# Two attention decodes on one core: the last weights in a staircase of transfers

## The chip, the cores and the metric

The kernel runs on one core of one Trainium2 chip. The metric is the device time of one execution in microseconds. An execution with the profiler gives the trace from which all rows in this document come.

## What is computed

There are two independent attention blocks, A and B, of the same size. Each decodes a single token against a cache of 8192 positions, with 32 heads of 128, and the two results are put side by side. All inputs are bfloat16.

```python
B, Sq, D = 1, 1, 512
H, Sk, Dh = 32, 8192, 128
q = (x @ wq).reshape(B, Sq, H, Dh).transpose(0, 2, 1, 3)
scores = einsum("bhqd,bhkd->bhqk", q, k_cache) * (Dh ** -0.5)
o = einsum("bhqk,bhkd->bhqd", softmax(scores), v_cache)
y = o.transpose(0, 2, 1, 3).reshape(B, Sq, H * Dh) @ wo
out = concatenate([yA, yB], axis=-1)
```

K and V of one block are 64 MB each, wq and wo 4 MB each, so that some 285 MB (decimal) go from HBM into the core once. The output has 1024 numbers.

## The kernel before, in words

Four heads of one block are handled together; I call this a quad. There are 16 quads (`NM`), numbers 0 to 7 of A and 8 to 15 of B. Each of the four heads takes 32 of the 128 partitions, and a partition holds 256 positions (`T`) of its head. So K or V of a quad is one transfer of 8 MB, 64 KB for each partition.

For a quad n the steps are: `plan_mul` multiplies K by the broadcast q on DVE, in four chunks of 64 columns; `plan_red` sums over the head dimension, first on PE with the identity as weights (L342), then on DVE (`plan_sr`, L353); `plan_max`, `plan_gmax` and `plan_exp` (L390, on ACT) make the softmax's numerators `pt`; `plan_sum` (L395) the denominators; `plan_pv` (L411) takes 256 column tiles of V as weights, with the four columns of `pt` as moving data; `plan_o` (L421) scales the result into `oD`. PV of quad n-1 is written between the chunks of quad n. K has two buffers, V has one.

All large loads are issued by SP, in the order in which `load_...` is called, and each waits on SP for its buffer. K of quad n+1 waits for the last reduction of quad n-1, and V of quad n waits for the end of PV of quad n-1. In the last round there is no K left to load; there the projection weights wo take the buffer of the K that was reduced last but one (`wo_sb`, L192): all of A and the first `BEFORE` groups of B are issued in K's place, ahead of the last V, and the other groups of B after it (L503 to L506, L536 and L537).

`WOG` (L169) divides the heads of wo into groups, (first head, number of heads). A group is one transfer (`load_wo`, L286) of 128 partitions: a row for each partition, n heads x 512 columns x 2 bytes, 1 KB for each head. In the matmul with wo the contraction runs over the partition, p, and partition p has n neighbouring rows of wo and not one row of each head. Therefore `oD` is regrouped for each group of more than one head (`plan_relayout`, L440): a masked product on DVE (L449), one matmul with a selection matrix (L454) and a copy (L458) into `o2`. `plan_wo` (L461) then does four matmuls for each head with wo as weights (L469), all accumulating in one PSUM bank, after a wait for the group's transfer (`s_wo[a][g]`). A group of one head is taken straight from `oD`. `plan_y` (L476) copies the sum into `yT` on DVE, and `plan_out` (L480) transposes it, copies it and stores it by SP.

Before the change B has eight groups, of 8, 4, 4, 8, 4, 2, 1 and 1 heads. The first two are issued ahead of the last V, the six others after it. The last V comes in three transfers (`VLAST`, L172), of columns 0 to 128, 128 to 192 and 192 to 256, each with a semaphore of its own, and `plan_pv` is cut at the same columns for each quad. The order on PE at the end is: the projection of A and of B's first two groups; the regrouping of the groups that need no head of the last quad; PV of quad 15 by parts; `plan_o`; the group after `BEFORE`; the regrouping of the group that does need the last quad (heads 28 and 29); the remaining groups in order; `yT`, out.

PE runs quads 1 to 15 as a loop over one body of instructions. PV of quad 15 takes the same body a second time with the rest left out (L581 to L599).

Of the kernel before, what the change touches and what calls it, by code (L numbers as in the profile page):

```python
# [11 lines left out]
P = 128  # L12
# [11 lines left out]
class _Plan:  # L24
# [15 lines left out]
    def op(self, eng, fn, ctr=None, needs=(), inc=1):  # L40

        for m in needs:
            self.wait(eng, m)
        self.prog[eng].append((fn, ctr, inc))
        if ctr is None:
            return None
        ctr.n += inc
        return ctr, ctr.n
# [81 lines left out]
def bass_concat_heads__mha_block_cached__gqa_block_cached__decode_kernel(  # L130
# [18 lines left out]
    NA = 2  # L149
# [9 lines left out]
    T = Sk // HP  # L159
    assert T == 256  # L160
    QA = H // G
    NM = NA * QA
    NK = 2
    CT = 64
    NCH = T // CT
    DW = 512 // CT
    assert Dh % DW == 0

    WOG = [[(0, 32)], [(0, 8), (8, 4), (12, 4), (16, 8), (24, 4), (28, 2), (30, 1), (31, 1)]]  # L169
    BEFORE = 2  # L170
    RG = [32, 16, 8, 4, 2]
    VLAST = (0, T // 2, T // 2 + CT, T)  # L172

    with ExitStack() as st:
        ec = st.enter_context
# [8 lines left out]
        def flat(ap):  # L184
            return ap.rearrange("p t d -> p (t d)")
# [6 lines left out]
        wo_sb = [flat(kn[:, KW])[:, a * W:(a + 1) * W].rearrange("p (j n) -> p j n", n=NOUT)  # L192
                 for a in range(NA)]
# [37 lines left out]
        def ctr(name):  # L231
            return _Ctr(nc, st, name)

        s_x = ctr("s_x")
        s_w = [ctr("s_w%d" % a) for a in range(NA)]
        s_wo = [[ctr("s_wo%d%d" % (a, i)) for i in range(len(WOG[a]))] for a in range(NA)]
        s_k = [ctr("s_k%d" % i) for i in range(NK)]
        s_v = [ctr("s_v%d" % i) for i in range(len(VLAST) - 1)]
        s_out = ctr("s_out")
# [3 lines left out]
        def dma(eng, dst, src, c, needs=()):  # L243
            return op(eng, lambda e: e.dma_start(dst, src), c, needs, inc=16)  # L244
# [21 lines left out]
        k_in, v_in, wq_in, wo_in = {}, {}, {}, {}  # L266
        red_done, pv_done, q_done, wo_done = {}, {}, {}, {}
# [9 lines left out]
        def load_v(n, cuts=(0, T)):  # L277
            dst, src = flat(vn[:]), quad(vs, n)
            v_in[n] = [(t0, dma("SP", dst[:, t0 * Dh:t1 * Dh], src[:, t0 * Dh:t1 * Dh], s_v[i],
                                [q_done[1] if n == 0 else pv_done[n - 1]]))  # L280
                       for i, (t0, t1) in enumerate(zip(cuts, cuts[1:]))]
# [4 lines left out]
        def load_wo(a, g):  # L286
            h0, n = WOG[a][g]
            src = wos[a][h0 * Dh:(h0 + n) * Dh, :].rearrange("(p j) n -> p (j n)", p=P)
            wo_in[a, g] = dma("SP", wo_sb[a][:, h0:h0 + n, :].rearrange("p j n -> p (j n)"), src,
                              s_wo[a][g], [red_done[NM - 2, NCH - 1]])  # L290


        for a in range(NA):
# [80 lines left out]
        def plan_exp(n):  # L374
            def bc(e):
                r = None
                for h in range(G):
                    r = e.matmul(bmp[:, 0:1], hrow[0:1, h, :], gm[0:1, h:h + 1],  # L378
                                 start=(h == 0), stop=(h == G - 1))
                return r  # L380
            m = op("PE", bc, c_pe, [i_pool, gm_done[n], nb_done.get(n - 1)])
            nb_done[n] = op("ACT", lambda e: e.activation(  # L382
                negb[:, n:n + 1], bmp[:, 0:1], AF.Copy, scale=-scale), c_act, [m])
            wait("ACT", nb_done[n])
            wait("ACT", pv_done.get(n - 1))
            wait("ACT", r_done.get(n - 1))
            wait("ACT", i_pool)
            for h in range(G):
                q = slice(h * HP, (h + 1) * HP)
                p_done[n] = op("ACT", lambda e, h=h, q=q: e.activation(  # L390
                    pt[q, :, h], s_sb[q, :], AF.Exp, bias=negb[q, n:n + 1],
                    scale=scale, accum_out=rsum[q, h:h + 1]), c_act)

        def plan_sum(n):
            m = op("PE", lambda e: e.matmul(misc[:, 0:G], ones_f[:], rsum[:],  # L395
                                            start=True, stop=True), c_pe,
                   [p_done[n], misc_free[0]])
            r_done[n] = misc_free[0] = op("DVE", lambda e: e.reciprocal(
                rinv[:, n, :], misc[:, 0:G]), c_dve, [m])

        def plan_pv(n, t0, t1):
            for t, landed in v_in[n]:
                if t < t1:
                    wait("PE", landed)
            wait("PE", p_done[n])
            wait("PE", o_done.get(n - 1))

            def mm(e):
                r = None
                for t in range(t0, t1):  # L410
                    r = e.matmul(acc[:, 0:G], vn[:, t, :], pt[:, t, :],  # L411
                                 start=(t == 0), stop=(t == T - 1))
                return r
            if t1 == T:
                pv_done[n] = op("PE", mm, c_pv)
            else:
                op("PE", mm)
# [22 lines left out]
        def plan_relayout(*groups):  # L440
            assert len(groups) <= 2
            made = []
            for a, g in groups:
                h0, n = WOG[a][g]
                z = z_n[0] % 2
                z_n[0] += 1
                s = P // n
                zv = zb[:, z, :].rearrange("p (h s) -> p h s", s=s)
                made.append((a, g, h0, n, z, op("DVE", lambda e, a=a, h0=h0, n=n, s=s, zv=zv: e.tensor_tensor(  # L449
                    zv, oD[:, a, h0:h0 + n].unsqueeze(2).broadcast_to([P, n, s]),  # L450
                    mask[n][:, None, :].broadcast_to([P, n, s]), ALU.mult),
                    c_dve, [sel_ready[n], o_done[a * QA + (h0 + n - 1) // G], z_free.get(z)])))
            for a, g, h0, n, z, m in made:
                z_free[z] = op("PE", lambda e, n=n, z=z: e.matmul(  # L454
                    z_ps[z][:, 0:n], zb[:, z, :], jsel[n][:], start=True, stop=True),
                    c_pe, [m, z_read[z][0]])
            for a, g, h0, n, z, m in made:
                o2_ready[a, g] = z_read[z][0] = op("DVE", lambda e, a=a, h0=h0, n=n, z=z: e.tensor_copy(  # L458
                    o2[:, a, h0:h0 + n], z_ps[z][:, 0:n]), c_dve, [z_free[z]])

        def plan_wo(a, g):  # L461

            h0, n = WOG[a][g]

            def mm(e):
                r = None
                for j in range(h0, h0 + n):
                    for i in range(NQ):
                        r = e.matmul(qyp[:, i:i + 1], wo_sb[a][:, j, i * P:(i + 1) * P],  # L469
                                     (o2 if n > 1 else oD)[:, a, j:j + 1], start=(j == 0 and i == 0),  # L470
                                     stop=(j == H - 1 and i == NQ - 1), skip_group_check=True)
                return r
            wo_done[a] = op("PE", mm, c_pe, [o2_ready[a, g] if n > 1 else o_done[a * QA + h0 // G],
                                            wo_in[a, g], qy_free[0]])
# [23 lines left out]
        for n in range(NM):  # L498
            if n >= L0:
                cuts[n].append(len(pl.prog["PE"]))  # L500
            if n + 1 < NM:
                load_k(n + 1)
            else:  # L503
                load_wo(0, 0)
                for g in range(BEFORE):
                    load_wo(1, g)  # L506
# [13 lines left out]
            else:  # L520
                cuts[n].append(len(pl.prog["PE"]))
                plan_sum(n - 1)
                for t0, t1 in zip(VLAST, VLAST[1:]):
                    plan_pv(n - 1, t0, t1)
# [6 lines left out]
            plan_exp(n)  # L531
            load_v(n, VLAST if n == NM - 1 else (0, T))
        cuts[NM].append(len(pl.prog["PE"]))
        NB = len(WOG[1])
        early = [g for g, (h0, n) in enumerate(WOG[1]) if h0 + n <= H - G]
        for g in range(BEFORE, NB):  # L536
            load_wo(1, g)  # L537
        z_read[1][0] = gm_done[NM - 1]
        plan_relayout((0, 0), (1, 0))
        plan_relayout((1, 1))  # L540
        plan_wo(0, 0)
        plan_y(0)
        for g in range(BEFORE):
            plan_wo(1, g)
        plan_relayout(*[(1, g) for g in early[BEFORE:BEFORE + 2]])
        plan_relayout(*[(1, g) for g in early[BEFORE + 2:]])
        wait("PE", misc_free[0])
        cuts[NM].append(len(pl.prog["PE"]))
        plan_sum(NM - 1)
        for t0, t1 in zip(VLAST, VLAST[1:]):  # L550
            plan_pv(NM - 1, t0, t1)
        cuts[NM].append(len(pl.prog["PE"]))
        plan_o(NM - 1)
        plan_wo(1, BEFORE)
        plan_relayout(*[(1, g) for g in range(len(early), NB) if WOG[1][g][1] > 1])
# [5 lines left out]
        for name, at in (("SP", block.sync), ("PE", block.tensor), ("ACT", block.scalar),  # L561
                         ("DVE", block.vector), ("POOL", block.gpsimd)):
            @at
            def _(e, name=name):
# [7 lines left out]
                final = _steps(prog[cuts[L1][1]:cuts[L1][2]])  # L572
                assert len(final) == b - a == len(VLAST)
                for k, (ws, it) in zip(range(a, b), final):
# [53 lines left out]
```

## Time and profile before

| What | Value |
|---|---|
| Median of two executions | 668.25 us (668.13 and 668.37) |
| The profiled execution | 668.1 us, its span 666.3 us |
| Granted PE clock over the span | 0.767 |
| Read from HBM | 285.21 MB, 428 GB/s over the span |
| Last K landed, first multiply of quad 15 | 604.9 us |
| Last V issued, three transfers | 631.58 us |
| Six groups of wo of B issued after it | from 632.90 us, 5.40 us in all |
| PV of quad 15, 192 tiles and 64 tiles | from 651.35 us for 5.29 us, from 657.50 us for 1.87 us |
| Last quad's `oD` | 659.40 us |
| `yT` of B | 663.91 us |
| Output store issued | 664.74 us |

Times within an execution are microseconds from the start of the span. The span ends with the last instruction; the profiled execution's own time is 1.8 us longer than its span. "Busy" is the time in which an engine had an instruction in it. A line such as `661.04 1.01 PE L469 ... x32 [0.82 <-DMA ...]` means: from 661.04 us on, for 1.01 us, PE ran 32 matmuls of line 469, and had stood idle for 0.82 us until a DMA came in. `SPq` is SP's queue of DMA issues. In the table by windows each row is a stretch of the span, with the busy time of each engine in it, the granted PE clock, the busy share of the 16 DMA engines and what they moved.

### The profile page before, as it was taken

The page shows a single profiled execution, that of the slowest core. Times are in us where ns is not written, and L with a number is a line of the kernel's source. Part 1 is how long each engine was busy: PE and PEld are TensorE (multiplying, and loading weights), DVE is VectorE, ACT ScalarE, POOL GpSimd, SP SyncE. Part 2 cuts the span into 40 slices and gives each one's busy share as a digit, 9 for nine tenths or more (in the row PEclk, how much of TensorE's full clock was granted, in tenths as well). Part 3 has the DMA queues.
Part 4 walks back from the last instruction along what each step waited for, and adds up shares of the span by engine and source line. Part 5 has one row for each costly group of instructions (what it writes and reads, how often), then busy time and mean ns, then how long its engine had stood idle before and what let it go on. Part 6 is the DMA issues. An engine that isn't in the chain of part 4 may idle for free.

```text
span 666.3 us, 12270 instructions
## 1 busy us (share of the span) xinstructions
PE 445.5 (67%) x5648; PEld 254.5 (38%) x5648; DVE 340.8 (51%) x219; ACT 62.4 (9%) x151; POOL 2.8 (0%) x15
## 2 busy tenths in 40 slices
PE   2065876848487594848659484865948386685866
PEld 1022352625244261614426161442626144252646
DVE  1095807466381836638082663809256481925611
ACT  1002002020201002020200202020020202002020
POOL 1000000000000000000000000000000000000000
PEclk9998767879787765978776587877658797765875
DMA  9999999999999999999999999999999999999997
GB/s 378 441 441 438 438 435 441 409 425 441 433 433 441 437 441 437 409 433 441 433 433 441 433 441 429 421 433 441 429 437 437 437 441 421 425 437 437 408 430 301
DMA packets 6509, 285.34 MB, mean 428 GB/s; under 512 B 738, under 2 KB 996, under 8 KB 1508
## 3 DMA queue, kind: packets, MB, share of 16 engines
q1 hardware_dynamic: 6496, 285.22, 99.2%
q8 instruction: 6, 0.10, 0.1%
q14 instruction: 3, 0.02, 0.0%
q10 hardware_dynamic: 4, 0.00, 0.0%
HBM read 285.21 MB, written 0.00 MB: 428 GB/s over the span
## 4 chain that ended last, share of the span: by engine, by line
DMA 57%; PE 28%; DVE 12%; issue 2%; SPq 1%; another core or an unknown queue 0%; ACT 0%
DMA kn<-in_B_k_cache_dram 20%; DMA kn<-in_A_k_cache_dram 18%; PE rps L342 17%; DVE kn L333 11%; PE acc L411 10%; DMA vn<-in_A_v_cache_dram 10%; DMA vn<-in_B_v_cache_dram 5%; DMA kn<-in_B_wo_dram 4%; DVE s_sb L353 1%; SPq L244 1%; PE qyp L315 0%; DVE m L359 0%; PE misc L395 0%; PE mtp L365 0%
## 5 line engine op out<-in xcount | busy, mean ns | idle before, releaser
L342 PE MATMUL rps<-kn,ident 128*128 128x512 bf16 x1024 | 297.8, 460 | 164.6 <-DVE kn L333 164.6
L333 DVE TENSOR_TENSOR kn<-kn,qbc 128x8192 bf16<-128x8192 bf16 x64 | 281.4, 4418 | 92.1 <-DMA kn<-in_A_k_cache_dram 53.6
L342 PEld LDWEIGHTS rps<-kn,ident 128*128 128x128 bf16 x1024 | 113.5, 115 | 335.9 <-issue 263.6
L411 PE MATMUL acc<-pt,vn 128*128 128x4 bf16 x4096 | 109.0, 165 | 7.8 <-issue 5.0
L411 PEld LDWEIGHTS acc<-pt,vn 128*128 128x128 bf16 x4096 | 108.6, 100 | 8.4 <-issue 6.0
L353 DVE TENSOR_REDUCE s_sb<-rps 128x64 f32<-128x512 f32 x64 | 44.0, 688 | 115.6 <-PE rps L342 115.6
L390 ACT ACTIVATE pt<-s_sb,negb 32x256 bf16<-32x256 f32 x64 | 54.8, 857 | 2.1 <-ACT negb L382 0.2
L382 ACT ACTIVATE negb<-bmp 128x1 f32<-128x1 f32 x16 | 2.7, 171 | 529.0 <-PE bmp L378 529.0
L421 DVE TENSOR_TENSOR oD<-acc,rinv 128x4 bf16<-128x4 f32 x16 | 2.6, 162 | 92.0 <-PE acc L411 92.0
L378 PE MATMUL bmp<-gm,hrow 1*128 1x1 f32 x128 | 17.6, 255 | 6.0 <-DVE gm L368 6.0
L378 PEld LDWEIGHTS bmp<-gm,hrow 1*128 1x128 f32 x128 | 16.3, 195 | 10.7 <-DVE gm L368 10.0
L365 PE MATMUL mtp<-ident_f,m 128*1 128x128 f32 x32 | 6.1, 271 | 19.8 <-DVE m L359 19.8
L390 ACT ACTIVATION_READ_ACCUMULATOR pt<-s_sb,negb 32x1 f32 x64 | 15.9, 248 | 0.0
L365 PEld LDWEIGHTS mtp<-ident_f,m 128*1 128x1 f32 x32 | 1.4, 81 | 27.7 <-DVE m L359 27.7
L469 PE MATMUL qyp<-o,kn 128*128 128x1 bf16 x248 | 7.6, 165 | 5.0 <-issue 3.4
L315 PE MATMUL qyp<-vn,xb 128*32 128x512 bf16 x64 | 6.0, 504 | 5.4 <-DMA vn<-in_A_wq_dram 3.9
L469 PEld LDWEIGHTS qyp<-o,kn 128*128 128x128 bf16 x248 | 7.1, 103 | 5.4 <-issue 4.1
L368 DVE TENSOR_REDUCE gm<-mtp 1x4 f32<-1x128 f32 x16 | 4.5, 278 | 7.5 <-PE mtp L365 7.5
L395 PEld LDWEIGHTS misc<-rsum,ones_f 128*128 128x128 f32 x32 | 6.2, 197 | 2.9 <-issue 0.7
L359 DVE TENSOR_REDUCE m<-s_sb 128x1 f32<-128x256 f32 x16 | 6.7, 420 | 0.5
L323 ACT CAST qbc<-qyp 128x512 bf16<-128x512 f32 x4 | 2.3, 586 | 42.8 <-PE qyp L315 42.8
L297 PE MATMUL misc<-ones_bf,kn 1*128 1x128 bf16 x4 | 0.6, 302 | 8.2 <-DMA kn<-in_B_x_dram 8.2
(36 smaller groups left out, 26.5 us busy)
## 6 DMA issues: line engine op xcount, KB each, us to landing
vn<-in_A_wq_dram SPq DMA_DIRECT2D x1, 4096.0 KB, 12.2
vn<-in_B_wq_dram SPq DMA_DIRECT2D x1, 4096.0 KB, 40.3
kn<-in_A_wo_dram SPq DMA_DIRECT2D x1, 4096.0 KB, 35.3
vn<-in_B_v_cache_dram SPq DMA_DIRECT2D x1, 4096.0 KB, 15.9
vn<-in_B_v_cache_dram SPq DMA_DIRECT2D x2, 2048.0 KB, 22.6
kn<-in_B_wo_dram SPq DMA_DIRECT2D x2, 1024.0 KB, 32.5
kn<-in_B_wo_dram SPq DMA_DIRECT2D x3, 512.0 KB, 28.4
kn<-in_B_wo_dram SPq DMA_DIRECT2D x1, 256.0 KB, 28.6
```

What stands on the lines that cost most here:

```text
L244: return op(eng, lambda e: e.dma_start(dst, src), c, needs, inc=16)
L315: r = e.matmul(qyp[hh * HP:(hh + 1) * HP, :].rearrange("p (i d) -> p i d", d=Dh), xb[:, a, c, hh * HP:(hh + 1) * HP], w, start=(c == 0), s ...
L333: mul_done[n, c] = op("DVE", lambda e: e.tensor_tensor(k, k, qbc[:, n:n + 1, :].broadcast_to([P, CT, Dh]), ALU.mult), c_mul, [k_in[n], qbc ...
L342: r = e.matmul(rps[:, c % 2, :].rearrange("p (t d) -> p t d", d=DW), ident[:], kn[:, i0, c * CT:(c + 1) * CT, i * DW:(i + 1) * DW], start= ...
L353: sr_done[n, c] = op("DVE", lambda e: e.tensor_reduce(s_sb[:, c * CT:(c + 1) * CT], rps[:, c % 2, :].rearrange("p (t d) -> p t d", d=DW), ...
L359: m_done[n] = op("DVE", lambda e: e.tensor_reduce(m1[:], s_sb[:], AX.X, ALU.max), c_dve, [sr_done[n, NCH - 1]])
L365: m = op("PE", lambda e: e.matmul(mtp[0:1, 0:P], m1[:], ident_f[:], start=True, stop=True), c_pe, [m_done[n], i_identf, gm_done.get(n - 1)])
L378: r = e.matmul(bmp[:, 0:1], hrow[0:1, h, :], gm[0:1, h:h + 1], start=(h == 0), stop=(h == G - 1))
L390: p_done[n] = op("ACT", lambda e, h=h, q=q: e.activation(pt[q, :, h], s_sb[q, :], AF.Exp, bias=negb[q, n:n + 1], scale=scale, accum_out=rs ...
L395: m = op("PE", lambda e: e.matmul(misc[:, 0:G], ones_f[:], rsum[:], start=True, stop=True), c_pe, [p_done[n], misc_free[0]])
L411: r = e.matmul(acc[:, 0:G], vn[:, t, :], pt[:, t, :], start=(t == 0), stop=(t == T - 1))
L469: r = e.matmul(qyp[:, i:i + 1], wo_sb[a][:, j, i * P:(i + 1) * P], (o2 if n > 1 else oD)[:, a, j:j + 1], start=(j == 0 and i == 0), stop=( ...
```

## The change

B's wo has three groups now: 16, 8 and 8 heads. The group of 16 is issued ahead of the last V, in one transfer; the first group of 8 after V in one transfer of 128 partitions; the last group of 8 in 15 transfers, each of consecutive partitions, of 15, 14, 13, 12, 11, 10, 9, 9, 8, 7, 6, 5, 4, 3 and 2 partitions. All 15 add to one semaphore, and the matmuls of that group wait for the sum of all. Each partition's row is 8 KB. The last V comes in two transfers, columns 0 to 192 and 192 to 256, and PV is cut there for each quad.

On PE and DVE, the first 16 heads are regrouped together with A and projected ahead of PV of quad 15; heads 16 to 23 are regrouped ahead of it and projected after it; heads 24 to 31, which have the last quad among them, are regrouped after it, and then projected with 32 matmuls.

```diff
-    WOG = [[(0, 32)], [(0, 8), (8, 4), (12, 4), (16, 8), (24, 4), (28, 2), (30, 1), (31, 1)]]
-    BEFORE = 2
+    WOG = [[(0, 32)], [(0, 16), (16, 8), (24, 8)]]
+    LASTP = (15, 14, 13, 12, 11, 10, 9, 9, 8, 7, 6, 5, 4, 3, 2)
+    BEFORE = 1
     RG = [32, 16, 8, 4, 2]
-    VLAST = (0, T // 2, T // 2 + CT, T)
+    VLAST = (0, T - CT, T)
...
         def load_wo(a, g):
             h0, n = WOG[a][g]
             src = wos[a][h0 * Dh:(h0 + n) * Dh, :].rearrange("(p j) n -> p (j n)", p=P)
-            wo_in[a, g] = dma("SP", wo_sb[a][:, h0:h0 + n, :].rearrange("p j n -> p (j n)"), src,
-                              s_wo[a][g], [red_done[NM - 2, NCH - 1]])
+            dst = wo_sb[a][:, h0:h0 + n, :].rearrange("p j n -> p (j n)")
+            p0 = 0
+            for k in LASTP if a == NA - 1 and g == len(WOG[a]) - 1 else (P,):
+                wo_in[a, g] = dma("SP", dst[p0:p0 + k, :], src[p0:p0 + k, :],
+                                  s_wo[a][g], [red_done[NM - 2, NCH - 1]])
+                p0 += k
+            assert p0 == P
...
         plan_relayout((0, 0), (1, 0))
-        plan_relayout((1, 1))
         plan_wo(0, 0)
         plan_y(0)
-        for g in range(BEFORE):
-            plan_wo(1, g)
-        plan_relayout(*[(1, g) for g in early[BEFORE:BEFORE + 2]])
-        plan_relayout(*[(1, g) for g in early[BEFORE + 2:]])
+        plan_wo(1, 0)
+        plan_relayout(*[(1, g) for g in early[BEFORE:]])
         wait("PE", misc_free[0])
```

## The prediction, made before the result

> **What bounds the kernel now.** I read the page first (engine shares, the slices, the queues, the chain of waits), then the table by windows over the end, then the timeline of the SP queue and of PE from 645 us on.
>
> ```profile
> PE 445.5 (67%) x5648; PEld 254.5 (38%) x5648; DVE 340.8 (51%) x219; ACT 62.4 (9%) x151; POOL 2.8 (0%) x15
> ...
> DMA  9999999999999999999999999999999999999997
> GB/s 378 441 441 438 438 435 441 409 425 441 433 433 441 437 441 437 409 433 441 433 433 441 433 441 429 421 433 441 429 437 437 437 441 421 425 437 437 408 430 301
> ...
> HBM read 285.21 MB, written 0.00 MB: 428 GB/s over the span
> ```
>
> No compute engine is busy for more than 67% of the span, and the DMA engines are above 90% in every slice but the last. The kernel is a stream of 285 MB, and its end is the end of that stream plus what hangs on the last bytes. So a change can act in three ways: more or fewer bytes, a pause in the stream, or a different last stretch. The windows show the last stretch.
>
> ```profile
> core 0: us, PE busy (x) PEld busy (x) DVE busy (x) ACT busy (x) POOL busy (x), PEclk, DMA share, GB/s
> ...
> 652.00:656.00 4.00, 4.00 (x155) 4.00 (x153) 0.00 (x0) 0.00 (x0) 0.00 (x0) 0.50 0.98 415
> 656.00:660.00 4.00, 2.89 (x102) 2.73 (x100) 0.45 (x2) 0.00 (x0) 0.00 (x0) 0.50 0.99 407
> ...
> 661.25:661.50 0.25, 0.25 (x16) 0.25 (x13) 0.00 (x0) 0.00 (x0) 0.00 (x0) 0.50 0.86 307
> 661.50:661.75 0.25, 0.25 (x15) 0.25 (x13) 0.00 (x0) 0.00 (x0) 0.00 (x0) 0.50 0.49 188
> ...
> 662.50:662.75 0.25, 0.25 (x15) 0.25 (x12) 0.00 (x0) 0.00 (x0) 0.00 (x0) 0.50 0.43 152
> 662.75:663.00 0.25, 0.14 (x6) 0.06 (x3) 0.00 (x0) 0.00 (x0) 0.00 (x0) 0.50 0.14 45
> 663.00:663.25 0.25, 0.21 (x8) 0.25 (x8) 0.00 (x0) 0.00 (x0) 0.00 (x0) 0.50 0.03 8
> ```
>
> The column before the last is the share of the 16 DMA engines that is busy. It falls from 0.99 to about one half at 661.5, stays there for over 1 us and is out at 663.1: half of the engines finish near 661.3, the other half 1 to 2 us later, though each has the same bytes. The completion marks in the trace say the same: those of the last transfer run from 661.67 to 663.56, eight within the first 0.3 us and seven in the last 0.6. The page's queue list has nine small instruction loads (six of 16 KB, three of 8 KB), and the spread grows in the marks just where one of them falls; at 41 us it is 0.35, from 525 us on it is 2.0. I call an engine's distance from the first its lag. If the load were even over time, all would end near 662.5.
>
> ```profile
> 631.58 1.28 SPq L244 DMA_DIRECT2D vn<-in_B_v_cache_dram  x3
> 632.90 5.40 SPq L244 DMA_DIRECT2D kn<-in_B_wo_dram  x6
> ...
> 661.04 1.01 PE L469 MATMUL qyp<-o,kn 128*128 128x1 bf16 x32 [0.82 <-DMA kn<-in_B_wo_dram]
> 662.31 1.08 PE L469 MATMUL qyp<-o,kn 128*128 128x1 bf16 x24 [0.25 <-DMA kn<-in_B_wo_dram]
> 663.29 0.58 PE L469 MATMUL qyp<-oD,kn 128*128 128x1 bf16 x8
> 664.13 0.27 PE L481 MATMUL bmp<-ident,yT 128*8 128x128 bf16 x1 [0.26 <-DVE yT L477]
> ```
>
> All transfers of the end are queued by 638.3, more than 20 us before they land, and PE follows them. Heads 16 to 23 are complete at 661.04, and the four matmuls of head 31 start at 663.61 (PE timeline of the last half microsecond). yT on DVE starts at 663.91, 0.30 after that.
>
> **The change part by part.** The bytes are the same.
>
> *Heads 8 to 15 move ahead of V.* They wait for the same reduction as now (issued at 598.65 and after) and are 0.5 MB more ahead of V at 631.58. V needs no cover: the marks put the end of what is ahead of it at 635.7 to 637.7, so the stream does not pause now and would not after. Cost 0; without that backlog a late V would cost its whole delay.
>
> *V in two parts, 192 and 64 columns.* PE can start the first 192 tiles only when 6 MB have landed, not 4. By the stream that is near 653.4, two microseconds later than now (651.35); 5.29 for the 192 and 1.87 for the 64 end at 660.7 against 659.4 now. Then come oD (0.16), 32 matmuls of heads 16 to 23 (1.01) and the relayout of the last eight heads (0.29 + 0.17 + 0.16, beside them): done by 662.1. The last weights land after 663.4 in every case below, so this costs 0; it would begin to cost if they landed before 662.
>
> *Fewer rows.* Rows of 16 and 8 KB take the place of rows of 4, 2 and 1 KB. In the packet records every row costs about 0.008 us beyond its bytes at 27 GB/s (1 KB in 0.046, 8 KB in 0.312) and a completion 0.010. Up to head 23 an engine goes from 56 rows and 7 completions to 32 and 4: 0.2 us less. So the engine that lags most has head 23 at 660.8 and not 661.04, and the first engine, lag 2.0 less, at 658.8.
>
> *Fifteen transfers for the last eight heads.* A row (one partition, eight heads) is 8 KB. By the 656 to 660 window an engine moves 407/16 = 25.4 GB/s, so a row with its completion is 0.32 us. An even share is 8 rows, 2.6 us. Transfers of 15 down to 2 partitions can be spread in two ways. If one begins where the last one left off, every engine gets about 8 rows again: 660.8 + 2.6 = 663.4 on the last. If each begins at the same engine, that one has 15 rows, the next 15, 14, 13 and so on, and the sixteenth none: 4.8 us on the fullest. The nearest rows are the store of 8 partitions (16 packets in its window: 8 of data and 8 of completion, so one engine for a partition) and the transfers of 128, whose lag pattern stays from one to the next, so that shares do not wander from engine to engine. I take the fixed order. [...]
>
> What then decides is the lag of the engines with 15, 15, 14 and 13 rows. If all four are early ones: 658.8 + 0.3 + 4.8 = 663.9. If one is the latest: 660.8 + 4.8 = 665.6. The trace does not number the engines, and about half of them lag by 1.5 to 2.0; that none of four lags has a chance of about one in 25 if order and lag have nothing to do with each other. I take one with 15 rows and a lag of 1.6: 665.2, which is 1.6 after 663.61. The staircase is simply steeper (0 to 4.8 us) than the lag that it could level (0 to 2.0).
>
> *Issue.* SP issues 15 transfers where it issued five small ones. At 0.33 to 0.43 each that is 5 to 6.5 us from 633.3 on, and done by 640, hidden by V's traffic until 658.8; it could be 1.7 us each before it showed. Nothing waits behind them on SP but the final store. POOL and ACT issue nothing here.
>
> *After the last landing.* Now 0.30 from the last release of PE to yT, four matmuls. Then 32 matmuls: 1.01 (the row at 661.04) + 0.04: 0.75 more. PE's rows are 8 times as many behind one wait, since the wait is for all fifteen transfers.
>
> Sum: +1.6 + 0.75 = +2.35 on the profiled execution's 668.1 (its span 666.3 and 1.8 around): 670.5. The median of the two runs shown is 668.25, 0.15 more. The bounds of this case are 663.9 and 665.6, so 669.1 to 670.9.
>
> **The rivals.**
>
> *Neighbouring partitions take turns.* [...] Chance 0.32.
>
> *The queue holds too few transfers.* The sixth wo transfer's issue took 3.02 us instead of 0.43 (the SP rows), with some ten transfers in flight. If the limit counts transfers, about six of the fifteen get out early and nine wait for one another: 9 x 0.43 on 660.8, and 0.8 from issue to first packet as with the store: 665.5 or more plus the rest of the rows, about 672 to 675 us. Against: if the limit counts rows, 36 + 30 on the fullest engine are fewer than the 78 there now. Chance 0.06.
>
> *The shares are even after all* (transfers rotate, or the order of the lags fits the stairs in part): 663.4, or 668.1 - 0.2 + 0.75 = 668.7 us. Chance 0.08.
>
> *The stairs fit the lags.* All engines end near 662.2 (the mean 662.5 less 0.3), 1.4 sooner: 668.1 - 1.4 + 0.75 = 667.5. The fullest engine's 15 rows from 658.8 speak against it: 663.6 at the earliest. Chance 0.02.
>
> **How the numbers follow.** The forecast has 0.52: 670.5, range of its own 669.1 to 670.9. The range is 668.6 to 677.5: it holds the forecast, the even case, the queue case and about two thirds of the turns (in step and near it are left out). About 2%, 13 us, is what a measurement of this kernel can tell from no change. Slower by more than that needs nearly all neighbours in step: 0.05. Faster by that would need an end at 655, below the time that the bytes take at 441 GB/s (647) plus start and end: 0.01. Within 2%: 0.94.
>
> **What would show it.** Right: the DMA share falls by steps over 4 to 5 us, from about 659 to 665, and not over 2; PE's 32 last matmuls start near 665 after a wait for wo, and yT about 1.05 later; the packets of the end still take 0.31 us for 8 KB. Neighbours in turn would show as the DMA share near 0.9 at far less than 400 GB/s, rows of 0.6 us or more. A short queue would show in SP's issues going on past 658. Wrong altogether would be an end of traffic before 663.4, or V or its matmuls as the last wait.

## The result, and the profile after

| | before | after |
|---|---|---|
| Median | 668.25 us | 672.64 us (672.46 and 672.83) |
| Ratio to before | | 1.0067, 95% interval 1.0050 to 1.0083 |
| Profiled execution, span | 668.1, 666.3 us | 672.46, 670.7 us |

The changed kernel is slower by 0.7%, 4.4 us. That is clear of the interval and far below 2%. The page shows no more bytes and no busier compute engine; the stream is as full as before until the last slice, where 301 GB/s have become 186:

```profile
PE 440.2 (66%) x5645; PEld 253.2 (38%) x5645; DVE 339.8 (51%) x213; ACT 62.4 (9%) x151; POOL 2.8 (0%) x15
...
DMA  9999999999999999999999999999999999999995
GB/s 375 438 438 439 435 428 438 438 438 438 434 430 430 430 422 434 438 434 434 430 438 434 438 438 438 434 426 434 430 422 434 434 434 438 430 438 438 421 415 186
...
HBM read 285.21 MB, written 0.00 MB: 425 GB/s over the span
```

The table by windows of the changed kernel's end (the last two columns are the busy share of the DMA engines and their GB/s):

```profile
656.00:658.00 2.00, 2.00 (x81) 2.00 (x78) 0.00 (x0) 0.00 (x0) 0.00 (x0) 0.50 0.99 414
658.00:659.00 1.00, 1.00 (x43) 1.00 (x40) 0.00 (x0) 0.00 (x0) 0.00 (x0) 0.50 1.11 328
659.00:660.00 1.00, 1.00 (x43) 1.00 (x41) 0.00 (x0) 0.00 (x0) 0.00 (x0) 0.50 0.71 172
660.00:661.00 1.00, 0.59 (x23) 0.51 (x19) 0.33 (x2) 0.00 (x0) 0.00 (x0) 0.50 0.82 213
661.00:662.00 1.00, 0.00 (x0) 0.00 (x0) 0.12 (x1) 0.00 (x0) 0.00 (x0) 0.50 0.85 205
...
664.00:665.00 1.00, 0.03 (x1) 0.00 (x0) 0.17 (x1) 0.00 (x0) 0.00 (x0) 0.50 0.34 123
665.00:666.00 1.00, 0.00 (x0) 0.00 (x0) 0.00 (x0) 0.00 (x0) 0.00 (x0) 0.50 0.12 41
666.00:667.00 1.00, 0.00 (x0) 0.00 (x0) 0.00 (x0) 0.00 (x0) 0.00 (x0) 0.50 0.04 16
```

Two things are to be seen. From 664 on the share falls by steps to 0.12, two engines, and 0.04, the end of one: the stairs, as forecast. But from 659 to 662 the engines are 0.7 to 0.85 busy and move only 172 to 213 GB/s; at 0.99 busy they moved 414. A busy engine moves about 60% of what it did. In the packet records, which give each DMA packet's start, duration and size but not its engine, rows of 8 KB mostly take 0.44 to 0.58 us between 659 and 662.5 (0.77 at most), against 0.31 before 658 and for most rows again after 664.5. The forecast had 0.31 throughout.

The chain at the end, in the timelines of SP, PE and DVE:

```profile
631.26 0.80 SPq L245 DMA_DIRECT2D vn<-in_B_v_cache_dram  x2
632.11 5.92 SPq L245 DMA_DIRECT2D kn<-in_B_wo_dram  x16
...
653.58 7.01 PE L417 MATMUL acc<-pt,vn 128*128 128x4 bf16 x256 [2.49 <-DMA vn<-in_B_v_cache_dram]
662.99 1.01 PE L475 MATMUL qyp<-o,kn 128*128 128x1 bf16 x32 [2.40 <-DMA kn<-in_B_wo_dram]
663.86 0.17 PE L460 MATMUL mtp<-jsel,zb 128*128 128x8 bf16 x1
667.31 0.99 PE L475 MATMUL qyp<-o,kn 128*128 128x1 bf16 x32 [3.28 <-DMA kn<-in_B_wo_dram]
668.34 0.16 DVE L483 CAST yT<-qyp 128x4 bf16<-128x4 f32 x1 [4.11 <-PE qyp L475]
668.56 0.27 PE L487 MATMUL bmp<-ident,yT 128*8 128x128 bf16 x1 [0.26 <-DVE yT L483]
```

PE's last release moved from 663.61 to 667.31, 3.70 us. yT starts at 668.34, 1.03 after the release instead of 0.30: 0.73 us. The two make 4.43, and the span grew by 4.4. Heads 16 to 23, one transfer of 128 partitions in both kernels, are complete at 662.99 and not at 661.04: the slow stretch hits that transfer's last rows too, in the engines that lag.

### The profile page after: what moved, and what is told of

Read it like the earlier page. It is cut to its first block, busy times and chain, and to the rows that moved or that the text cites. A ratio compares the mean times of both kernels' runs of the same rounds, so it can differ in the third digit from the quotient of the medians.

```text
span 670.7 us, 12251 instructions
## 1 busy us (share of the span) xinstructions
PE 440.2 (66%) x5645; PEld 253.2 (38%) x5645; DVE 339.8 (51%) x213; ACT 62.4 (9%) x151; POOL 2.8 (0%) x15
## 4 chain that ended last, share of the span: by engine, by line
DMA 65%; PE 23%; DVE 9%; issue 1%; SPq 1%; ACT 0%
DMA kn<-in_B_k_cache_dram 20%; DMA kn<-in_A_k_cache_dram 18%; DMA vn<-in_A_v_cache_dram 14%; PE rps L348 13%; PE acc L417 10%; DMA vn<-in_B_v_cache_dram 9%; DVE kn L339 8%; DMA kn<-in_B_wo_dram 4%; SPq L245 1%; DVE s_sb L359 1%; PE qyp L321 0%; PE qyp L475 0%; ACT qbc L329 0%; PE misc L401 0%; PE bmp L487 0%
## 5 line engine op out<-in xcount | busy, mean ns | idle before, releaser
L348 PE MATMUL rps<-kn,ident 128*128 128x512 bf16 x1024 | 292.1, 453 | 167.9 <-DVE kn L339 167.9
L348 PEld LDWEIGHTS rps<-kn,ident 128*128 128x128 bf16 x1024 | 111.8, 113 | 335.2 <-issue 259.4
```

The source lines that it names most:

```text
L348: r = e.matmul(rps[:, c % 2, :].rearrange("p (t d) -> p t d", d=DW), ident[:], kn[:, i0, c * CT:(c + 1) * CT, i * DW:(i + 1) * DW], start= ...
```

## The experiments

Each is the changed kernel with the lines edited that the cuts below show. Where `LASTP` is a list of pairs of slices, `load_wo` goes through the pairs, destination and source partitions of a transfer, in place of counting up. Medians of before on the same chip lay between 668.12 and 668.27. "Rows" are 8 KB packets of wo in the packet records.

| Run | Last eight heads of B | us | Ratio to before, 95% interval |
|---|---|---|---|
| one128 | one transfer | 668.6 | 1.0005 (0.9996 to 1.0015) |
| one128_v3 | one transfer, V in three | 668.7 | 1.0009 (1.0000 to 1.0018) |
| fine_end | 4, 2, 1, 1 heads, 128 partitions each | 667.96 | 0.9997 (0.9988 to 1.0006) |
| near16 | 8 x 16 neighbours | 671.31 | 1.0046 (1.0029 to 1.0062) |
| apart16 | 8 x 16, 8 apart | 671.37 (670.49 to 672.65) | 1.0051 (1.0035 to 1.0068) |
| step4 | 8 x 16, 4 apart | 671.66 | 1.0053 (1.0034 to 1.0071) |
| mix7 | 8 x 16, seven of them 7 apart | 671.05 | 1.0043 (1.0026 to 1.0059) |
| mix7_src_near | same, read from neighbouring rows | 670.89 | 1.0040 (1.0026 to 1.0054) |
| halves | 2 x 64 | 671.82 | 1.0053 (1.0037 to 1.0070) |
| stairs_apart | stairs, 8 apart | 672.1 | 1.0057 (1.0041 to 1.0074) |
| far8 | 16 x 8, 4 apart | 671.38 | 1.0047 (1.0031 to 1.0063) |
| near8 | 16 x 8 neighbours | 673.21 (672.4 and 674.02) | 1.0075 (1.0054 to 1.0095) |

**Is it the split at all?**

```diff
-    LASTP = (15, 14, 13, 12, 11, 10, 9, 9, 8, 7, 6, 5, 4, 3, 2)
+    LASTP = (128,)
```

> The last eight heads in one transfer of 128 partitions, all else as changed. Stairs theory (what was lost lies in 15 rows on one DMA engine) and neighbours theory (what was lost lies in rows to neighbouring partitions that take turns) agree: the whole loss in the stream goes, and only the 32 matmuls behind the last wait stay, 668.25 - 0.2 + 0.75 = 668.8 us. A third theory, that the loss came from the other parts (V in two transfers, 16 heads ahead of it), would leave it near 672.

668.6. The whole loss in the stream is gone. This run's windows:

```profile
659.00:660.00 1.00, 1.00 (x44) 1.00 (x41) 0.00 (x0) 0.00 (x0) 0.00 (x0) 0.50 1.00 418
660.00:661.00 1.00, 0.69 (x26) 0.60 (x23) 0.24 (x2) 0.00 (x0) 0.00 (x0) 0.50 0.94 393
661.00:662.00 1.00, 0.95 (x33) 0.95 (x33) 0.21 (x1) 0.00 (x0) 0.00 (x0) 0.50 0.45 188
```

Its last matmuls with wo, in PE's timeline:

```profile
663.57 0.99 PE L475 MATMUL qyp<-o,kn 128*128 128x1 bf16 x32 [1.47 <-DMA kn<-in_B_wo_dram]
```

The rate stays near 400 GB/s until half of the engines are done. The last release is at 663.57, 0.04 from that of before.

**The other parts of the change.** V in three parts again, with that one transfer:

```diff
-    LASTP = (15, 14, 13, 12, 11, 10, 9, 9, 8, 7, 6, 5, 4, 3, 2)
+    LASTP = (128,)
...
-    VLAST = (0, T - CT, T)
+    VLAST = (0, T // 2, T // 2 + CT, T)
```

> The last eight heads in one transfer, and V in three transfers again. If V in two transfers is hidden, as forecast: 668.6 us, as with two. If the later start of PV cost something: down to 668.3.

668.7, the same: V's parts are hidden. And the end in smaller groups of whole height, with one transfer for each:

```diff
-    WOG = [[(0, 32)], [(0, 16), (16, 8), (24, 8)]]
-    LASTP = (15, 14, 13, 12, 11, 10, 9, 9, 8, 7, 6, 5, 4, 3, 2)
+    WOG = [[(0, 32)], [(0, 16), (16, 8), (24, 4), (28, 2), (30, 1), (31, 1)]]
+    LASTP = (128,)
```

> The changed kernel's 16 heads ahead of V and V in two transfers, then 8, 4, 2, 1 and 1 heads in transfers of 128 partitions, as the kernel before ends. Both theories: no row takes turns and no engine has more than another, four matmuls stand behind the last wait; fewer rows than before, -0.23: 668.0 us. Against the kernel with eight heads in one transfer (668.6) it should be 0.6 to 0.75 less; if it is not, the matmuls behind the last wait were priced wrongly.

667.96, 0.64 less than one128 and 0.74 less than one128_v3, which ran on the same chip: that is the price of 32 instead of four matmuls behind the last wait. Against before it is 0.2 less, as forecast for the fewer rows, but the interval holds 1: no shown gain. No version tried beats the kernel before beyond its interval.

**Stairs or turns?** Eight even transfers of 16 partitions, neighbours or 8 apart, and the stairs with partitions 8 apart:

```diff
+    LASTP = (16,) * 8                                                 # near16
+    LASTP = [(slice(r, P, 8), slice(r, P, 8)) for r in range(8)]      # apart16
...
+    STEP = [(15, 1), (14, 2), (13, 3), (12, 4), (11, 5), (10, 6), (9, 7), (9, 7)]
+    LASTP = [(slice(r + 8 * i, r + 8 * (i + k) - 7, 8),) * 2 for r, (m, n) in enumerate(STEP)
+             for i, k in ((0, m), (m, n)) if k]
```

> Eight transfers of 16 neighbouring partitions: every DMA engine has 8 rows again, but 16 neighbours are written at a time. Stairs theory: as with one transfer, 668.8 and 0.1 for the completions, 668.9 us. [...]

> Eight transfers of 16 partitions that lie 8 apart, 8 rows for each DMA engine. Stairs theory: 668.9 us. [...] If small transfers cost something by their number (eight instead of one), it shows here above the kernel with one transfer.

> The same stairs, 16 rows on the fullest DMA engine down to none, in 16 transfers, but the partitions of a transfer lie 8 apart. If the stairs alone made the loss: 672.6 + 0.3 for the sixteenth row = 672.9 us. If neighbours added to it: the forecast of the stairs without turns, 670.5 + 0.3 = 670.8 us, and rows at 0.31 us in the trace.

near16: 671.31; with no stairs at all, 2.7 us are lost. So stairs alone are not the cause. But apart16, in which no two partitions of a transfer are neighbours, lost as much (671.37), and stairs_apart, at 672.1, hardly gained. "Neighbours" was too narrow: rows to partitions 8 apart are slow too. apart16's windows:

```profile
659.00:660.00 1.00, 1.00 (x44) 1.00 (x42) 0.00 (x0) 0.00 (x0) 0.00 (x0) 0.50 1.06 221
660.00:661.00 1.00, 0.69 (x26) 0.60 (x23) 0.24 (x2) 0.00 (x0) 0.00 (x0) 0.50 1.01 221
```

All 16 engines busy, 221 GB/s, 53% of 418. Its rows between 659 and 660.5 are 0.61 to 0.65 us, twice 0.31; from then to 662.5 their median is 0.50.

That left four causes: rows to certain partitions, neighbours or not, slow one another when they are written at once; a transfer with one row for an engine is slow by itself (eight completions instead of one); an engine is slow on partitions it does not have in a transfer of 128; neighbouring rows are slow to read. The next runs are for these.

```diff
+    LASTP = [(slice(b + r, b + r + 29, 4),) * 2 for b in range(0, P, 32) for r in range(4)]   # far8
+    LASTP = (8,) * 16                                                                         # near8
+    LASTP = [(slice(b + r, b + r + 61, 4),) * 2 for b in (0, 64) for r in range(4)]           # step4
```

> Sixteen transfers of 8 partitions that lie 4 apart: one row for each of 8 DMA engines, the other 8 engines have nothing; the fullest have 16 rows. [...] Theory that one row for each engine and transfer is slow by itself: rows at 0.5 to 0.6 as in the runs with 16, 16 x 0.55 = 8.8 us, 673 to 675 us. Theory that an engine is slow on partitions that are not its own in a transfer of 128: half of the rows at 0.6, 671 to 673 us.

> The same with 8 neighbouring partitions in each transfer. [...]

far8's windows, and its last release in PE's timeline:

```profile
660.00:661.00 1.00, 0.65 (x24) 0.57 (x22) 0.35 (x2) 0.00 (x0) 0.00 (x0) 0.50 0.50 205
661.00:662.00 1.00, 0.98 (x33) 0.89 (x33) 0.11 (x1) 0.00 (x0) 0.00 (x0) 0.50 0.56 229
662.00:663.00 1.00, 0.00 (x0) 0.00 (x0) 0.17 (x1) 0.00 (x0) 0.00 (x0) 0.50 0.48 197
...
666.00 0.99 PE L472 MATMUL qyp<-o,kn 128*128 128x1 bf16 x32 [4.02 <-DMA kn<-in_B_wo_dram]
```

near8's:

```profile
660.00:661.00 1.00, 0.65 (x25) 0.56 (x22) 0.28 (x2) 0.00 (x0) 0.00 (x0) 0.50 0.59 180
661.00:662.00 1.00, 0.00 (x0) 0.00 (x0) 0.18 (x1) 0.00 (x0) 0.00 (x0) 0.50 0.48 131
662.00:663.00 1.00, 0.58 (x21) 0.58 (x22) 0.00 (x0) 0.00 (x0) 0.00 (x0) 0.50 0.51 205
663.00:664.00 1.00, 0.47 (x18) 0.38 (x15) 0.17 (x1) 0.00 (x0) 0.00 (x0) 0.50 0.52 213
```

In both a share of 0.5 says that 8 of 16 engines work, one for a partition. In far8 they move about 200 GB/s, 25 each, and every row is 0.31: one row for each engine and transfer is not slow, and neither is an engine on other partitions than its usual ones, since each has 16 where a transfer of 128 (128 rows, 16 completion marks) gives it eight. Its last release is at 666.00, where the stairs' arithmetic puts an engine with 16 rows and the largest lag (660.8 + 16 x 0.32 = 665.9); its time is 671.38. In near8, with the same rows for each engine, 131 GB/s at 0.48 make 0.48 us for a row on average, and then from 662 on the full rate is there again (205 GB/s at 0.51): rows are back to 0.31 while 8 engines are still busy. What ends the slowing is not shown; no record says which engine writes what. Its time, 673.21, is 1.8 above far8. The theories of single rows and of an engine's own partitions give both runs the same time.

> [...]

671.66, with 16 partitions in a transfer, 4 apart as the eight of far8 are. Two of its windows:

```profile
660.00:661.00 1.00, 0.46 (x18) 0.37 (x14) 0.46 (x2) 0.00 (x0) 0.00 (x0) 0.50 0.97 221
...
662.00:663.00 1.00, 0.61 (x23) 0.62 (x24) 0.00 (x0) 0.00 (x0) 0.00 (x0) 0.50 0.60 131
```

With all engines busy 221 GB/s are moved. The rows' median is 0.61 us between 659.5 and 660 and 0.51 to 0.60 in the half microseconds from there to 662.5. That is nearly twice the 0.31 of far8.

> [...] Theory of one row for each engine and transfer, and theory of an engine's own partitions: as with partitions 8 apart, 671.3 us.

> The same destinations, 7 apart, but the 16 rows of wo that a transfer reads are neighbours in HBM (so the rows come into other partitions than the matmul has them, and the last eight heads of B are projected with the wrong rows). If it matters what is read, 16 rows of one 128 KB stretch at a time: above the kernel with rows 7 apart, up to 671.3 us. If only the destination matters: the same as that one within 0.5 us.

```diff
+    LASTP = [(slice(112, 128),) * 2] + [(slice(r, r + 106, 7),) * 2 for r in range(7)]    # mix7
+    LASTP = [(slice(112, 128),) * 2] + [(slice(r, r + 106, 7), slice(16 * r, 16 * r + 16)) for r in range(7)]
```

What is read made no difference: 671.05 and 670.89. mix7's time is the one that the theories of single rows and of an engine's own partitions gave, but far8 speaks against both. Rows at a distance of 7 are as slow as at a distance of 8: 213 GB/s at 0.96 between 660 and 661 make 0.59 us for a row. The engines are up to 2 us, six rows, apart, so rows of different transfers are written at once; whether these slow one another is not shown. Nor do the runs show why near16, all neighbours, took no longer than apart16, with none (671.31 and 671.37).

A limit of some 200 to 270 GB/s on all engines together, for transfers of fewer partitions, would fit the windows with 16 busy engines. It does not fit what follows them. In step4 between 662 and 663 the share is 0.60, about ten engines, which move 131 GB/s in all, and yet their rows take 0.58 us (median); in far8 eight engines move 205 GB/s with rows of 0.31. In near8, too, rows are slow at 131 GB/s. So it is not the sum that slows these rows.

Another limit could be tried: on completions, of which the runs with 16 have eight for each engine.

```diff
+    LASTP = (64, 64)
```

> Two transfers of 64 partitions, 0 to 63 and 64 to 127: four rows for each of 16 DMA engines in each, so two completions for an engine where the runs with 16 had eight, and one row for a transfer nowhere. [...] Theory of a limit on completions, or on transfers with a single row for an engine (all the runs with 16 rows at a time stood near 220 GB/s, and so did 8 engines at full rate): nothing left of it, rows at 0.31 us and 668.7 us.

671.82, and not the 668.7 of a limit on completions, with two completions for an engine:

```profile
659.00:660.00 1.00, 1.00 (x44) 1.00 (x42) 0.00 (x0) 0.00 (x0) 0.00 (x0) 0.50 0.97 213
660.00:661.00 1.00, 0.29 (x12) 0.21 (x8) 0.45 (x2) 0.00 (x0) 0.00 (x0) 0.50 1.08 246
...
662.00:663.00 1.00, 0.81 (x30) 0.81 (x31) 0.00 (x0) 0.00 (x0) 0.00 (x0) 0.50 0.68 147
```

Completions are not the cause, nor is it rows singly sent. Two transfers of half the height, with four rows for each engine, are as slow as eight of 16. The last row is like that of step4: eleven engines, 147 GB/s, rows of 0.61 us (median). Two halves in place of one transfer cost 3.2 us for 1 MB.

What is shown, then: in transfers of fewer than 128 partitions the last rows were slow in every run but far8, mostly 0.44 to 0.65 us where a row in a transfer of 128 takes 0.31. Neither the stairs, nor the completions, nor single rows, nor the sum of the traffic explain that, and the choice of partitions changes it (far8 against near8: 205 GB/s at 0.50 and 131 at 0.48, 671.38 and 673.21 us). What it is in that choice, no run isolates.

## Why the prediction was right and where it failed

The range (668.6 to 677.5) holds 672.64 and so does "within 2%". The likeliest case's own range, 669.1 to 670.9, does not: 1.7 us are missing. The wide range held because it had been drawn to take in part of the turns, not because the sum of 670.5 was right.

- *The stream carries the time; V, the early heads and the issues are hidden.* Right. PV starts at 653.58 (forecast 653.4), the 16 issues took 5.92 us and were over by 638.03, and one128_v3 puts V's parts at nothing. The rival of a short queue falls with the same row. Of heads 8 to 15 only 12 to 15 moved ahead of V, the 0.5 MB; 8 to 11 were there already.
- *Fewer rows, -0.2.* It agrees with fine_end (-0.2, inside its interval), so it is not contradicted and not shown.
- *Matmuls behind the last release, +0.75.* Measured 0.73 by the trace, 0.64 and 0.74 by fine_end against one128 and one128_v3.
- *The stairs are steeper than the lag.* Right. Followed back by end and start times, the packets that end last are 15 rows one behind the other, and from 664.2 on they take 0.31 to 0.33, with ever fewer others beside them. far8, whose rows stay at 0.31, has the size of the term by itself: 16 rows, last release at 666.00.
- *A row is 0.32 us, from the 656 to 660 window.* This step failed. That window has transfers of 128 partitions alone. In the changed kernel the 15 rows of the last engine begin at 661.11 and end at 666.72, 5.61 us and not 4.8. They also begin about 1.2 later than forecast: a lag of 1.6 puts the release of head 23 at 660.4, and a release comes some 0.5 after the last packet (660.52 and 661.04 before). The reasons are that its rows of heads 16 to 23 took 0.43 to 0.59 from 659.6 on, and that its lag was nearer 2.0 than 1.6. The two are 2.0 of the 2.1 us between 665.2 and 667.31.
- *The rival of the turns*, with 0.32, named the sign in the profile (a share near 0.9 far below 400 GB/s, rows of 0.6 us or more). The changed kernel has 0.71 to 0.85 at 172 to 213 GB/s, and rows of about 0.5 for a stretch of 3.5 us and not to the end: later they go back to 0.31. How many rows take turns at a time, which the upper end of the range was drawn from, no run shows; they show rows of up to about twice 0.31, and for part of the time. The place was also wider than "neighbours": apart16, step4 and halves have rows of about 0.6 us for 0.31 between 659.5 and 660.5. This rival deserved the larger chance, since the forecast's row time came from transfers of 128 partitions alone.

## What to carry to other kernels

Keep loads at the full 128 partitions, also where the DMA engines are to get uneven shares: every cut of the last 1 MB into transfers of fewer partitions cost 2.3 to 4.6 us here against one transfer of 128, and with 16 engines at work it about halved the rate for some 3 us. A rate taken from one transfer shape holds for that shape alone: 418 GB/s in one128 and 221 in apart16, both with all engines busy. Before levelling a lag, compare the step of the tool with the size of the lag: here 4.8 us of stairs against 2.0, in an order that nothing ties to the lags.

## What was not expected of the hardware

- The loss is not confined to the odd transfers. Heads 16 to 23, a full transfer, were complete 2 us later (662.99 against 661.04). With one128 and far8, whose next rows run at 0.31, they were complete at 661.05 and 660.93; so the late rows of that transfer are slow where the rows that the early engines have gone on to are.
- The spread between DMA engines comes from the kernel's own instruction loads: nine in 670 us, and each leaves one engine behind by about 0.6 us (8 KB) or 1.4 us (16 KB) for the rest of the stream. Before the change the first, of 16 KB, falls at 53.5 us, and the completion marks of one transfer, 0.35 apart at 41.7, are 1.7 apart at 61. One of 8 KB falls at 259.2, and a mark that was at most 0.36 behind the first at 254.6 is 0.91 behind it at 273.9. Before the end the spread is 2.0 us in the kernel before and 2.3 in the changed one.
- The slowing ends by itself: near8 went from 131 to 213 GB/s at about the same share of busy engines (0.48 and 0.52), with no change in what was asked of them.
